# A searched order for a fused attention and gated-MLP kernel: no elementwise work on GpSimd, one float32 product for the first sums of squares, new tables

## The chip, the cores and the metric

One core of one Trainium2 chip. The metric is the device time of one execution in microseconds, the median over runs. The core's engines are PE (TensorE, matmuls), DVE (VectorE), ACT (ScalarE), POOL (GpSimd) and SP (SyncE, which here issues DMAs).

## The reference

Two parts, in float32. Attention over 8 batches, 8 heads, 576 positions and 64 dimensions, with a mask of its own for each half of the heads; then a gated MLP over the 4608 tokens x 512 features that come out:

```python
scores = q @ k.T / sqrt(64)               # masked with -1e9:
#   heads 0-3: 0 <= row - col < 32        heads 4-7: row >= col and row % 32 == col % 32
attn = softmax(scores) @ v                # -> x, 4608 tokens x 512
xn = x / sqrt(mean(x*x) + 1e-6) * rms_g
g, val = xn @ w_gate, xn @ w_val          # 512 x 1536 each
out = (g * sigmoid(g) * val) @ w_out      # 1536 x 512
```

## The kernel before, in words

**Numbers.** A large product is made in three matmuls: each operand is split into a high part (a cast to fp32r) and a low part (source minus high part), and high x high, low x high and high x low are summed. `split` (L584) does it: a copy that casts, by ScalarE or VectorE (`copyop`, L576, `copy_to`, L579), and a subtraction by VectorE or GpSimd (`elementwise`, L573; the instruction is recorded at L589). The helper `elementwise` also makes the additions and subtractions of L1201, L1022, L1029, L748, L762, L886 and L995.

**Attention.** 32 units, each one pair of heads of one batch. `unit_s` (from L664) makes a unit's scores in blocks of 64 columns (L699, L705: 72 or 36 short matmuls), the mask and maximum (L737, L740), the subtraction of it (L748), the exponential (L749), the row sum (L750), its reciprocal (L753, L754), the scaling (L762) and the transpose (L763). `unit_o` makes the values (L784, L797) and evacuates them (`evac`) into the chunk's rows. Units 0 to 3 form the lead-in; the others are put into the MLP's stages at places that the tables WIN, SAT, OAT, PSAT and POAT name.

**The MLP.** Nine chunks of 512 tokens. Chunks 0, 1 and 2 are computed plainly: for each of 12 blocks u of the hidden dimension the gate product (`slot_g`, L1077; in chunk 0 the first at L1085), the value product (L1077), and with a lag the output product (`slot_o`, L1132), 12 matmuls each. During chunk 0 the weights are read, unpacked on ScalarE and VectorE (`convert_weights`, L981 to L995) and split. Chunks 3 to 8 run as three pairs (`pair_of_chunks`) with a scheme of seven block products in place of eight; a block's products are called "5", "6", "2", "3", "7", "1", "4" (L1244, six matmuls each), and the outputs (L1373) follow, while the next pair's operands are made (`first_x`, `other_x`). Each chunk's RMS factor needs the sum of squares over features: `square` squares and adds up, `rms` sums over partitions with a product by ones. For chunk 0 it is four float32 products by ones, one per block of 128 features (L869), that accumulate in bank a1; `root0` follows.

**Order.** Nothing is issued as it is written. Each operation is registered by `op(engine, cost, ...)` with its reads and writes; `also=` names other engines that may do it. `Plan.forward` then simulates the engines with these costs (`act(n)`, `dve(n)`, `pool(n)`, SCO and PVO for scores and values, LATC for the latency between engines, TAIL) and at each step issues, on the engine that is free first, the ready operation with the lowest due time. The due times (DUE) and the slots in on-chip memory (PLACE) are two long tables found by a search. From chunk 1 on PE's operations keep the order in which they are written (`plan.serial`). Where the plan sees PE idle for long in the lead-in, filling matmuls on zeros are put in (`fill`, L603). The bytes of the tables are not shown.

Of the kernel before, what the change touches and what calls it, by code (L numbers as in the profile page):

```python
# [25 lines left out]
P = 128  # L26
# [27 lines left out]
MOVE = 60  # L54
# [5 lines left out]
SCO = (1340.0, 1050.0)  # L60
PVO = (1450.0, 1220.0)
# [6 lines left out]
TRA = 170.0  # L68
# [15 lines left out]
    "4028384c00041410061c352d585c591a1e40570b1b5b32045d4e211a50232e3d5319520c283840040814341c0c39155d3c3001393a04442400564d2f"  # L84
    "5a481c202c5d1814243c3854560f4004515a5d58551c3c140c2c4b5440004f585d494a1c14401c4c405618512c4c565455384a54484b512f59525c48"
    "49574b56544e4c1c502f53544e0e2e182d514f4c0c185d554c5b18400c534e5d2e510e2d2e402e3850530d4f50542e383853502e0c544a515d4e4e50"
    "542f4e180e1c2e545355512e0c0e1c50515b0d0c1e402e57564855545953495c4a1d401f1c2e2e50515839112c584a1c5a581f4d5c28525c1e2e524a"
    "18583618180e505a321c5c513410501d0f4b4a3832081f505a321036342458510e1e13045a44300c1e3758230b515a330b421c2943250e3c1e070d54"
    "3d3e16035a26341a2440001b3727350130020542314552321f120a0904153f10064c49232c4420224e53415149203211214a56284e581f2a4e163958"
    "36154f1323121454484a0a202b47492006085b3f22524a214c2d0c17592c1815582a2f0f2256575145171c5311554812143f5d4c2c5151221f58064d"  # L90
    "1d5910190b3909082253365b380a0f4d580a575309412d5d3f23462f2a2d125b444539323817143b182d513a194d1f2f3a28583b53490b230f090c57"
    "394d045336135810452d2b44194712481f4d1d18581138393a460f383348475836464804093b3809321c5a030641573f512a19314442450210430c28"
    "13001e0e1a3d2b07353c585a57510d30253e034127323f51110634181b1c3705443104471d241f0f132833460c0029104558095a1a11511232430e42"
    "2b010602075d2a531e343c03273f351621150d495119045b114740133741314f1f264855181b24363e4c0c1a590f10010646580212535d3515280017"
    "3d333f1d1c424e0e302a522529324d2b564307444554055c470327040d3c2f5851145b12363953110a233534595c021e162013075a144149222d5819"
    "15232f4a505c4c08122c4717105d4b442e3951080d16062d0f2304542c242e2d0a092159201e16120850375c513b0522365d4b4035455419353e0408"
    "272f2c1a2f494b4720505c110308405d204b3b535d161e530c08063b412459075b2f51153c46532e114605010803454750151a455d2e02343e13513c"
    "442e4516081e590f084c530c16105144411508075b12590d44271322531550040554061940485249245d290e18304f1e1c1101434d28033c2625553e"
    "5644515b15591d2904414c1b3f1a1f31490200074e48590f2a3d151c404d11332b2a1e4353520c285127323c425515181d121005543113060056264f"
    "1a3b292325024c1a09142a015241581b5d19403f0f040d202b1e494853210c113430223e425c560e513718354f033c10503233392d543d5929271d1c"  # L100
    "2c052813241f0706124e3643314d002655042f5a2e0844565d47092544505c0b524b0a423b3a1646394a0c17394a3c233e035b35505a025725385d58"
    "14562a4b000f50114d4c0151305726561a3a0416340b36523e515c4742371b45352a4434554d50464351023b1438102658164708110b5d554056251b"
    "0441471544190c09585c4f183f44570155000b0a0e18305d36513e0b35231a31555c4f46265641553c15512e1455175d03173f180016223b31345001"
    "1a092f4735144218263e46041a572a373036580f40430c1102102b271e543f4e23252053410e1f032c3d070d18473601112f51580c483c292e2d2105"
    "1c55493754503e201d4f2559061302331f4232002a311618011030030c34124d403f4e430e0d232235563a50412855534902360f37262b3d073c5c13"
    "211131011e42592d2c330551062f0401555847"))
DUE = np.frombuffer(bytes.fromhex(
    "024d0cf7017e01760cb00d6201b300070040002b018f0d4e0002016c000400000008021800050001000e0290000f0003007300430032001d001a0036"
    "016200ce02090052007500420093015c00940187010f01070022002a00390051007e001003da007a00230018000d02c400460071017b006a00d30014"
    "00170020004a001b0006009c0129012801fc01c40120000a0030004e003e004700290013000b000c010d00e6022401ab0100000900d900fd02750304"  # L110
    "02d600db00e701f400f9015800e4012400c1013b00c2010800bd00cb0069016900ed0207013f025c019500ad02b0009b011c01a900be00dc00a700b7"
    "006600aa01a0005900ae00b6005c011f0249025e00b1020e0193020a027a041401a10159021e00bc01540148010201a8009101e20406028a016b0142"
    "010400d000c700f600bb011e00a300920065006400280045011600a6011a019c002c009f005e010c018801840189021402280223013a0095005b007c"
    "01660127012e0080004b01ba02c001b901e50084028c01c0025a0164021c01d702f2012c033d022f02d301ed015e0230020201a70179033002690123"
    "011905d100f700e100fa00ea027b01da02760305012f0021001e00150016005d01fd02c8017d035002df0027001900240054015b01be025d02330212"
    "01460242020501b0014001ef01d200ec00eb002d0055003b024e021b016001c8033201b40149028d0165019f024701b602ad014f0229018101470286"
    "0206020b0231029e025102a801f2021101c5029c014d026d03aa01c9025501ee014a01cd02950172024a028902fa026401ad01c2034701f002cb0201"
    "0194048a02b5027e023c028801cf030a01f7034f024f02b80284035d02ea01c7026f01ae011b019b022d016801f8019801510296018a01cb01c60334"
    "014301750294031d0267015a01fa027c01dc02a502bf00f200dd00ff02b600df014b01d001a2030d02d201a301b20243032703e102570291021a0241"
    "01f50244025601e1024501e301df020f028e028301ea028f0279019701ca02250208028702c900d4029f01bd0232013701800280018e0250020d01a4"  # L120
    "01d500cc01ff0266026c027d0220027802b20215013803b902dc016f026501de023701530260029b02a100c001d1006c019d023d02e5031501c1025f"
    "027001c302e2020c0183031901e9016e0392029801f901d80254018b03a102210234024b013902ac039502a901d403d2014401e401f602a202aa013d"
    "029200fb037701bf027301fb036c02ae018d016d012a02a300ca004f025b017001ec04f3026a00780088004c010b041d023a0353010601e0019e01db"
    "02fc034e03860367022c02b301a503e4033f01ce03ba00f501d302ca029d03110452029a01e7023902cd037502a6021f01e803410177028202c302ff"
    "037802f10309016a02a4031802b702d101cc01f30302026e039002be02f802d503830272026303100385035803e7035902c10217014c029302e000f1"
    "035603310344028b022202ab038a0337035a0487039c02d80322047803e00363034903f40306066a05c304ee05b303c5034502ec03ca0407031f0468"
    "047b02610372041e032e0271021d0131041902bd02360252019902de01b701350117041b04430238057404ef05b80641031a02b103b800f3032d0404"
    "02f3025803b201d604bb0321012b00d2013600c6026b00f40113015600a10394041f037a038404c5036d03e902ef03c00083008d031303680325008b"
    "02fb02da036b035b008e00720374049c060a052a056503bd03b6036003fe044d042c0411039a02f4052804480063035203b3040902e601aa03c8036a"
    "03b4046302f6034a0307023b038d034206cd04d0058f069703d102e903cb037003290371030f034d03ce04e102f902f0040c025901860134031b0155"  # L130
    "022701030105010900cd03c7028103a7009d04e80465037c017a0362009e00600477055b065a048805f403a403ef02cc035402ed03f0048403550533"
    "03c104e60379030e0328022b03570346054c047d03ee037d03bf043c00d6004900740079039d0076008900a0004d00350061038002ee0323003a04d3"
    "032f02ba03de03ed00820050045505f605e60666003403b002c204aa038c03f702d7023e0277041603a0038f03fa033c049b037f041c03d802a00396"
    "050e0423039e03120361043905ff0597055605fe053b054d042e03d50433045c043604a80494051e049a03eb030c039803e503ab0403039704790434"
    "04100435032a033a03e203bc035e044b030b0338019a025302460491017403c3037b02e4024003e303200457036f062b02e10572053005b2051003bb"
    "0369042100c9046103ae0301042403000482032c04660196013e01d9024802ce0216042b00d100fe00b20097041803e8046900d50483045d03d00387"
    "006200a2045f06ce06c3064906be03d30343057002a7043e055306d804f5044704d6046000570210015f022a043101330182015d019000bf00a900c8"
# [102 lines left out]
PEN = {"DVE": 0.0, "ACT": 0.0, "Pool": 0.0}  # L240
# [189 lines left out]
def attn_moe(ctx: ExitStack, tc: tile.TileContext, qz: bass.AP, qT: bass.AP, kT: bass.AP, vz: bass.AP, vl: bass.AP,  # L430
# [129 lines left out]
    def dve(n, rate=0.96):  # L560
        return 150 + n / rate
# [1063 lines left out]
```

## Time and profile before

| | |
|---|---|
| median of three runs | 935.15 us (935.1 to 937.07) |
| the profiled execution | 937.66 us, span 935.9 us |
| PE busy | 915.2 us (98%), 8406 matmuls |
| PE weight loads | 738.3 us (79%) |
| DVE busy | 709.0 us (76%), 1083 instructions |
| ACT busy | 478.8 us (51%), 824 instructions |
| POOL busy | 145.4 us (16%), 115 instructions |
| DMA | 209.08 MB, mean 223 GB/s |
| mean granted TensorE clock | 0.996 |

The span runs from the first to the last instruction of the profiled execution; the time also has what lies around it. Busy time is the time in which an engine has at least one instruction in work. In the slices of the page PE is at nine tenths or more in all but the first and the last of forty. The chain of work that ended last lies on PE for 91% of the span and on DVE for 5%. The first matmul starts at 1.64 us, PE's first stretch without a gap at 39.21, and the last matmul ends near 931.2 us; two copies and two stores of 128 KB follow it.

### The profile page before, as it was taken

To read this page: it belongs to the slowest core of one execution; us is meant where nothing else is said; L and a number is where in the kernel's file an instruction comes from. 1 tells how busy PE (TensorE), PEld (TensorE's weight loads), DVE (VectorE), ACT (ScalarE), POOL (GpSimd) and SP (SyncE) were. 2 spreads that over 40 slices of the span, in tenths; PEclk is the share of its full clock that TensorE was granted. 3 is DMA by queue.
4 is the path that set the end of the run, shared out by engine and by line. 5 is a ranking of instruction groups with operands and counts; after the bars stand their busy time and mean duration, and the time that the engine had idled before them with its cause. 6 is when DMAs were issued, how large, how long until landed. Compare 5 with 4: busy or idle time off the path is not lost.

```text
span 935.9 us, 20718 instructions
## 1 busy us (share of the span) xinstructions
PE 915.2 (98%) x8406; PEld 738.3 (79%) x8406; DVE 709.0 (76%) x1083; ACT 478.8 (51%) x824; POOL 145.4 (16%) x115
## 2 busy tenths in 40 slices
PE   7899999999999999999999999999999999999997
PEld 4587788887878788888887887888888878888886
DVE  5999988878898878875678989554689984347781
ACT  6797764355445445454456672443466633233530
POOL 0112300100141410301025211000141120010200
PEclk9999999999999999999999999999999999999999
DMA  9966737879769549795646659964444698624642
GB/s 344 363 254 248 258 141 259 285 254 312 248 225 324 177 146 329 244 314 167 203 125 196 215 184 329 346 192 139 124 123 156 209 374 297 202 67 132 214 140 79
DMA packets 122655, 209.08 MB, mean 223 GB/s; under 512 B 10816, under 2 KB 66368, under 8 KB 119488
## 3 DMA queue, kind: packets, MB, share of 16 engines
q1 hardware_dynamic: 121840, 207.17, 66.0%
q8 instruction: 66, 1.08, 0.5%
q10 hardware_dynamic: 720, 0.59, 0.2%
q14 instruction: 29, 0.24, 0.1%
HBM read 163.68 MB, written 44.04 MB: 222 GB/s over the span
## 4 chain that ended last, share of the span: by engine, by line
PE 91%; DVE 5%; DMA 2%; issue 1%; ACT 0%; ACTq 0%; SPq 0%; DVEq 0%
PE a L1244 16%; PE g L1244 11%; PE v L1244 10%; PE a L1132 10%; PE g L1077 10%; PE v L1077 10%; PE a L1373 8%; PE v L1373 4%; PE g L1373 4%; PE pair L699 2%; PE pair L784 2%; DVE bl L589 1%; DMA xq<-in_qz_dram 1%; PE pair L797 1%; DMA few<-in_gain_dram 1%
## 5 line engine op out<-in xcount | busy, mean ns | idle before, releaser
L581 ACT CAST bl<-bl 128x512 fp32r<-128x512 f32 (+1 forms) x171 | 113.1, 685 | 107.4 <-DVE bl L1201 27.5
L1244 PE MATMUL a<-bl,bl 128*128 128x512 f32 x637 | 159.5, 394 | 0.0
L589 DVE TENSOR_TENSOR bl<-bl,bl 128x512 fp32r<-128x512 f32 x186 | 136.7, 758 | 16.1 <-ACT bl L581 4.8
L1244 PEld LDWEIGHTS a<-bl,bl 128*128 128x128 f32 x637 | 118.2, 188 | 25.5
L589 POOL TENSOR_TENSOR bl<-bl,bl 128x512 fp32r<-128x512 f32 x34 | 50.9, 1501 | 386.2 <-ACT bl L581 107.1
L1132 PE MATMUL a<-bl,bl 128*128 128x512 f32 x432 | 110.8, 394 | 0.0
L1244 PE MATMUL g<-bl,bl 128*128 128x512 f32 x426 | 109.0, 390 | 0.0
L1077 PE MATMUL g<-bl,bl 128*128 128x512 f32 x408 | 106.2, 400 | 1.0 <-DVE bl L1095 1.0
L1077 PE MATMUL v<-bl,bl 128*128 128x512 f32 x420 | 106.7, 392 | 0.2 <-DVE bl L1112 0.2
L1244 PE MATMUL v<-bl,bl 128*128 128x512 f32 x413 | 106.4, 390 | 0.0
L1255 DVE TENSOR_TENSOR a<-a,bl 128x512 f32<-128x512 f32 x72 | 50.2, 697 | 57.5 <-PE a L1244 44.0
L1132 PEld LDWEIGHTS a<-bl,bl 128*128 128x128 f32 x432 | 79.9, 188 | 17.2 <-DVE bl L589 0.3
L1201 DVE TENSOR_TENSOR bl<-bl,bl 128x512 f32<-128x512 f32 x103 | 72.8, 716 | 27.1 <-ACT bl L1260 25.8
L1244 PEld LDWEIGHTS g<-bl,bl 128*128 128x128 f32 x426 | 79.8, 188 | 16.7
L1077 PEld LDWEIGHTS v<-bl,bl 128*128 128x128 f32 x420 | 79.0, 188 | 17.6 <-DVE bl L1112 0.6
L1077 PEld LDWEIGHTS g<-bl,bl 128*128 128x128 f32 x408 | 76.1, 190 | 18.8 <-issue 1.6
L1244 PEld LDWEIGHTS v<-bl,bl 128*128 128x128 f32 x413 | 77.5, 188 | 16.3 <-ACT bl L1251 0.2
L1373 PE MATMUL a<-bl,bl 128*128 128x512 f32 x298 | 71.4, 390 | 0.0
L1373 PEld LDWEIGHTS a<-bl,bl 128*128 128x128 f32 x298 | 55.8, 188 | 11.7
L1373 PE MATMUL g<-bl,bl 128*128 128x512 f32 x208 | 50.1, 391 | 1.4 <-DVE bl L1393 1.4
L583 DVE CAST bl<-bl 128x512 fp32r<-128x512 f32 (+1 forms) x86 | 42.2, 494 | 12.0 <-PE a L1373 2.7
L1373 PE MATMUL v<-bl,bl 128*128 128x512 f32 x208 | 49.9, 390 | 0.7 <-DVE bl L1393 0.7
(175 smaller groups left out, 1318.7 us busy)
## 6 DMA issues: line engine op xcount, KB each, us to landing
bl<-gvd SPq DMA_DIRECT2D x252, 256.0 KB, 4.2
gvd<-bl SPq DMA_DIRECT2D x72, 256.0 KB, 4.3
bl<-to SPq DMA_DIRECT2D x72, 256.0 KB, 4.2
bl<-wos SPq DMA_DIRECT2D x54, 256.0 KB, 3.4
bl<-wos SPq DMA_DIRECT2D x12, 1024.0 KB, 6.5
bl<-in_wgv_dram SPq DMA_DIRECT2D x11, 1024.0 KB, 6.1
vt<-in_vl_dram SPq DMA_DIRECT2D x24, 352.0 KB, 3.7
xk<-in_kT_dram SPq DMA_DIRECT2D x28, 288.0 KB, 4.5
```

Of the source, the lines that this page charges most:

```text
L581: nc.scalar.copy(out=o, in_=i)
L583: nc.vector.tensor_copy(out=o, in_=i)
L589: elementwise(CH, lambda e: both(e).tensor_tensor(out=lo.new(F32R), in0=src(), in1=hi.f32(), op=ALU.subtract), reads + [hi.key], [lo.key])
L699: nc.tensor.matmul(out=pr[at // CH][32 * r:32 * r + 32, at % CH:at % CH + KW], lhsT=tq()[hd, q0:q0 + 32], rhs=tk_()[hd, q0:q0 + KW], start ...
L784: nc.tensor.matmul(out=ends[r % 2][0][n][64 * h:64 * h + 64, at + 32 * lo:at + 32 * hi], lhsT=va()[32 * r:32 * r + 32, D * (6 * n + j):D * ...
L797: nc.tensor.matmul(out=pr[s][64 * h:64 * h + 64, 32 * lo:32 * hi], lhsT=va()[r:r + 32, D * kb:D * kb + D], rhs=pT[r:r + 32, 64 * kb - 32 * ...
L1077: nc.tensor.matmul(out=out_, lhsT=w.t[:, sl], rhs=x.t, start=(kc == 0 and i == 0), stop=(kc == KC - 1 and i == 2))
L1132: nc.tensor.matmul(out=acc[t], lhsT=x.t[:, sl], rhs=w.t, start=(u == 0 and i == 0), stop=(u == NU - 1 and i == 2))
L1201: elementwise(CH, lambda e: both(e).tensor_tensor(out=o.new() if fresh else o.t, in0=a.t, in1=b.t, op=how), [a.key, b.key], [o.key])
L1244: nc.tensor.matmul(out=banks[bk], lhsT=w, rhs=xs[k][y].t, start=start and k == 0 and i == 0, stop=stop and k == 1 and i == 2, skip_group_c ...
L1255: op("DVE", dve(CH), 0, lambda: nc.vector.tensor_tensor(out=banks[bk], in0=banks[bk], in1=t.t, op=ALU.add), reads=[t.key], writes=[bk])
L1373: nc.tensor.matmul(out=banks[bks[j]], lhsT=v, rhs=xs[k][y].t, start=start and k == 0 and i == 0, stop=stop and k == KT - 1 and i == 2, ski ...
```

## The change

- `elementwise`, and the squares, no longer offer GpSimd as an engine: `also=[]`. GpSimd keeps its memsets and one copy of one column (L969).
- Chunk 0's squares go the way of the other chunks: one square stays as the accumulator, the other three are added to it (by `elementwise`), and a single float32 product by ones makes the sum (`square`, with p == 3).
- In chunks 1 and 2 a unit's loads stay where they were and its scores come after the block's gate product (`slot_g`) in place of ahead of it; in chunk 0 as before. In the pairs the scores come after product "2" in place of "6", one product later.
- The planner's costs: `act`, `dve`, SCO, PVO, TRA, LATC, `evac`, `copyop` and others have new numbers; scores and values get a new figure `soon` (SOON) by which their results are taken as ready earlier. MOVE and SQP go.
- PLACE and DUE have new contents. They change which slot a tile lies in, the order on each engine, which engine does an operation with a choice, and where `fill` is put.

```diff
-SCO = (1340.0, 1050.0)
-PVO = (1450.0, 1220.0)
+SCO = (1400.0, 1200.0)
+PVO = (1525.0, 1310.0)
+SOON = ((209.0, 171.0), (313.0, 234.0))
-TRA = 170.0
+TRA = 95.0
-LATC = 150.0
+LATC = 45.0
...
-            done = s + cost + self.TAIL[e]
+            done = s + cost + self.TAIL[e] - self.soon[i]
...
     def act(n, psum=False):
-        return (170 if psum else 195) + n / 1.2
+        return (55 if psum else 95) + n / 1.2 + 70 * (n > CH)
     def dve(n, rate=0.96):
-        return 150 + n / rate
+        return 70 + n / rate
...
     def elementwise(cost, fn, reads, writes):
-        op("DVE", dve(cost), 0, fn, reads=reads, writes=writes, port=True, also=[("Pool", pool(cost), True)])
+        op("DVE", dve(cost), 0, fn, reads=reads, writes=writes, port=True, also=[])
...
-        if c == 0:
-            sq = take()
...
-            hold.append((p, sq))
-            while p == 3 and hold:
-                n, s = hold.pop(0)
-                op("PE", SUM, 0, lambda n=n, s=s: nc.tensor.matmul(out=acc[1], lhsT=ones1.broadcast_to([P, P]), rhs=s.t, start=n == 0, stop=n == 3),
-                   reads=["ones", "pv3", s.key], writes=["a1"], pad=acc[1] if n == 0 else None)
-                give(s)
-            return
...
-        op("ACT", act(CH), 0, fn, reads=[rt.key], writes=[sq.key], also=way("i", ("DVE", dve(CH), True), ("Pool", pool(CH), True)))
+        op("ACT", act(CH), 0, fn, reads=[rt.key], writes=[sq.key], also=way("i", ("DVE", dve(CH), True)))
...
+        if c == 0 and p == 3:
+            s = ssq.pop(0)
+            op("PE", SUM, 0, lambda: nc.tensor.matmul(out=acc[1], lhsT=ones1.broadcast_to([P, P]), rhs=s.t, start=True, stop=True),
+               reads=["ones", "pv3", s.key], writes=["a1"], pad=acc[1])
+            give(s)
...
-                    if m == "6":
+                    if m == "2":
                         attention_s(u)
...
                     load(i)
                     load_v(i)
+                    if c == 0:
+                        unit_s(i)
+            slot_g(c, u)
+            for i, a in zip(WIN[c], SAT[c]):
+                if a == u and c:
                     unit_s(i)
-            slot_g(c, u)
```

## Rows read from the trace of the kernel before

**Rows 1.** The page, busy: us (share of span) xinstructions.

```profile
PE 915.2 (98%) x8406; PEld 738.3 (79%) x8406; DVE 709.0 (76%) x1083; ACT 478.8 (51%) x824; POOL 145.4 (16%) x115
```

**Rows 2.** Waits of PE: line, who ended it, total us, times, longest.

```profile
PE pair L699 <- issue: 2.2, 1, 2.2
...
PE g L1373 <- DVE bl L1393: 1.4, 1, 1.4
...
PE g L797 <- issue: 1.1, 1, 1.1
...
PE g L1077 <- DVE bl L1095: 1.0, 1, 1.0
...
PE v L1373 <- DVE bl L1393: 0.7, 1, 0.7
PE pair L797 <- issue: 0.7, 1, 0.7
PE v L784 <- DVE bl L1112: 0.7, 1, 0.7
PE pair L784 <- issue: 0.5, 1, 0.5
```

**Rows 3.** Timeline: start, us, engine line op out<-in xcount [idle before <-releaser].

```profile
555.03 0.68 DVE L589 TENSOR_TENSOR bl<-bl,bl 128x512 fp32r<-128x512 f32 x1
...
558.47 4.68 POOL L589 TENSOR_TENSOR bl<-bl,bl 128x512 fp32r<-128x512 f32 x3 [27.50 <-ACT bl L581]
558.51 1.80 DVE L589 TENSOR_TENSOR bl<-bl,bl 128x512 fp32r<-128x512 f32 x1 [0.87 <-ACT bl L581]
...
561.93 1.77 DVE L589 TENSOR_TENSOR bl<-bl,bl 128x512 fp32r<-128x512 f32 x1
```

**Rows 4.** The page, costliest groups: the subtraction (busy, mean ns).

```profile
L589 DVE TENSOR_TENSOR bl<-bl,bl 128x512 fp32r<-128x512 f32 x186 | 136.7, 758 | 16.1 <-ACT bl L581 4.8
...
L589 POOL TENSOR_TENSOR bl<-bl,bl 128x512 fp32r<-128x512 f32 x34 | 50.9, 1501 | 386.2 <-ACT bl L581 107.1
```

**Rows 5.** Timeline of PE around 321 us.

```profile
320.63 0.76 PE L699 MATMUL pair<-xk,xq 64*32 64x64 f32 x52
323.55 0.41 PE L699 MATMUL pair<-xk,xq 64*32 64x64 f32 x20 [2.17 <-issue]
```

**Rows 6.** DMA from 321.0 to 321.2 us: queue, packets, MB, share.

```profile
q8 instruction: 1, 0.02, 29.3%
```

**Rows 7.** Chain that ended last, 320 to 340 us: start, us, what.

```profile
323.97 4.40 PE g L1077 x12
...
335.29 2.72 PE g L1077 x12
```

**Rows 8.** Windows: length, busy PE, PEld, DVE, ACT, POOL (xcount), PEclk, DMA, GB/s.

```profile
30.00:40.00 10.00, 8.51 (x104) 5.46 (x105) 9.62 (x11) 10.00 (x16) 0.00 (x0) 1.00 0.83 319
40.00:130.00 90.00, 88.79 (x759) 71.14 (x758) 83.24 (x103) 69.62 (x80) 21.22 (x10) 1.00 0.66 242
```

**Rows 9.** Timeline of PE: the fourth float32 product, two passes.

```profile
40.75 1.02 PE L869 MATMUL a<-bl,ones 128*128 128x512 f32 x2
```

**Rows 10.** Timeline from 264 us: one unit, probabilities to values.

```profile
269.67 2.37 DVE L753 TENSOR_SCALAR st<-st 128x9 f32<-128x9 f32 x1
...
275.36 0.77 DVE L763 STREAM_TRANSPOSE pT<-pp 128x576 f32<-128x576 f32 x1
...
276.98 0.27 PE L784 MATMUL pair<-pT,vt 32*64 32x64 f32 x1
```

**Rows 11.** Timeline of VectorE ahead of the values at 522.8.

```profile
513.81 1.78 DVE L589 TENSOR_TENSOR bl<-bl,bl 128x512 fp32r<-128x512 f32 x1
515.52 1.84 DVE L748 TENSOR_TENSOR pp<-pp,st 128x576 f32<-128x576 f32 x1
...
521.91 0.78 DVE L763 STREAM_TRANSPOSE pT<-pp 128x576 f32<-128x576 f32 x1
```

More of the change, by code (lines that the diff above doesn't have):

```diff
@@ L53 @@
 MID = 2
-MOVE = 60
 BYROW = ()
@@ L262 @@
     LAT = LATC
-    TAIL = {"PE": 165.0, "DVE": 90.0, "ACT": 110.0, "Pool": 60.0, "SP": 0.0}
+    TAIL = {"PE": 165.0, "DVE": 90.0, "ACT": 110.0, "Pool": 100.0, "SP": 0.0}
     def __init__(self):
@@ L278, in __init__, with op @@
         self.pads = []
+        self.soon = []
         self.owner, self.picked, self.uses = {}, [], []
-    def op(self, eng, cost, at, fn, reads=(), writes=(), bytes_=0, rel=0.0, lock=(), tab=None, port=False, chain=False, also=None, early=0.0, follow=None, pad=None):
+    def op(self, eng, cost, at, fn, reads=(), writes=(), bytes_=0, rel=0.0, lock=(), tab=None, port=False, chain=False, also=None, early=0.0, follow=None, pad=None, soon=0.0):
         i = len(self.ops)
         self.pads.append(pad)
+        self.soon.append(soon)
         self.early.append(early)
@@ L573, in elementwise @@
     def elementwise(cost, fn, reads, writes):
[L574 removed]
+        op("DVE", dve(cost), 0, fn, reads=reads, writes=writes, port=True, also=[])
     def copyop(fn, reads, writes):
[L577 removed]
+        op("ACT", act(CH), 0, fn, reads=reads, writes=writes, also=[("DVE", 340, True)])
     def copy_to(e, o, i):
@@ L717, in peak @@
                 nc.vector.tensor_scalar(out=mx, in0=mx, scalar1=0.125, scalar2=None, op0=ALU.mult)
-            op("DVE", dve(SW) + (170 if keys_ == [SK] else 330), 0, peak, reads=keys_, writes=[sk])
+            op("DVE", dve(SW) + (220 if keys_ == [SK] else 330), 0, peak, reads=keys_, writes=[sk])
             if i in HALFQ:
@@ L754, in recip @@
             nc.vector.reciprocal(out=su, in_=su)
-        op("DVE", 430, 0, recip, writes=[sk], port=True)
+        op("DVE", 400, 0, recip, writes=[sk], port=True)
         if i in ROWS:
@@ L801, in unit_o @@
             keys_ = ends[0][1] + ends[1][1]
-        op("PE", PVO[eight] + (SLOWV if i < 4 else 0), 0, values8 if eight else values, reads=tkeys + kv, writes=keys_ + ["pv3"] * (i == 3), pad=pr[1])
+        op("PE", PVO[eight] + (SLOWV if i < 4 else 0), 0, values8 if eight else values, reads=tkeys + kv, writes=keys_ + ["pv3"] * (i == 3), pad=pr[1], soon=SOON[eight][1])
         give(*held, *y)
@@ L847, in unit_o @@
                 n = z1 - z0
-                op("ACT", act(n, True) + MOVE * (len(moves) - 1), 0, evac, reads=ek, writes=list(dict.fromkeys(s.key for s, _, _ in moves)),
-                   also=way("e", ("DVE", dve(n) + 80 * (len(moves) - 1), False)))
+                op("ACT", len(moves) * 55 + n * (1 / 1.2 if p < 2 else 1.4), 0, evac, reads=ek, writes=list(dict.fromkeys(s.key for s, _, _ in moves)),
+                   also=way("e", ("DVE", len(moves) * 70 + n * (1 / 0.96 if p < 2 else 1.4), False)))
         square(b, p)
@@ L954, in copyop2 @@
     def copyop2(fn, reads, writes):
-        op("ACT", act(2 * CH), 0, fn, reads=reads, writes=writes, also=[("DVE", 150 + 2 * 274, True)])
+        op("ACT", act(2 * CH), 0, fn, reads=reads, writes=writes, also=[("DVE", 605, True)])
     raws = []
@@ L1459, in half @@
                     copy_to(e, (dst.new() if lead else dst.t)[:, sl], banks[P2[j]][:, sl])
-                op(e, 310, 0, half, reads=[P2[j]] + [dst.key] * (not lead), writes=[("oh", c, j, n)] + [dst.key] * lead)
+                op(e, act(256, True) if e == "ACT" else dve(256), 0, half, reads=[P2[j]] + [dst.key] * (not lead), writes=[("oh", c, j, n)] + [dst.key] * lead)
                 op("ACT" if n == 0 and not more else "SP", 600 if n == 0 else 430, 0, lambda sl=sl, dst=dst, q=q, j=j: (nc.sync if more else q).dma_start(
```

291 lines of the change are left out of this document (142 added, 149 removed).

## Prediction

> **What bounds the kernel now.** I read the page's busy shares first. PE is busy for 915.2 of 935.9 us, DVE for 709.0, POOL for 145.4 [rows 1]. The matmuls follow one another without a gap nearly everywhere, so apart from PE work that is taken out, all that can be won is PE's waits, the lead-in and the tail. The waits of PE come next, because they name who ended each one [rows 2]. Four of them, 1.4, 1.0, 0.7 and 0.7 us, end on a VectorE operation; two, 2.2 and 0.5 us, and three more in the lead-in (0.7 to 1.1 us) end on "issue", which means on nothing that the profile shows.
>
> Why is VectorE late in those four? The timeline ahead of the 1.4 us wait shows it [rows 3]. A subtraction of 512 columns takes 0.68 us at 555.03. At 558.47 GpSimd starts three of the same kind that last 4.68 us together, and beside them three VectorE operations in a row, each of 512 columns, take 1.80 to 1.77 us (the first and the last are shown). The two engines don't add up: what GpSimd works, VectorE loses in part. Over the run GpSimd takes 1.50 us for such a subtraction and VectorE's own 186 average 0.758 us [rows 4], 0.078 above the undisturbed one, which is 14.5 us on that line alone.
>
> The longest wait stands inside one unit's scores: 52 small matmuls go out, nothing for 2.17 us, then the other 20 of the same tile [rows 5]. They read the operands of the first 52, so it is not data. In the 0.2 us from 321.0, just ahead, the instruction queue carries one packet [rows 6]; I read the wait as PE running out of instructions after values and scores, two bursts of short matmuls with only six long ones between them. It costs twice: the next twelve matmuls take 4.40 us, twelve of the same kind later 2.72 [rows 7], a clock at half its level (1.2 instead of 2.4 GHz) for a while after the idle time.
>
> **The change part by part.** The sum is made against the profiled execution, 937.66 us with a span of 935.9 (1.8 lie around it); the median of the three runs is 935.15, 2.5 below, and I take the difference over to it.
>
> 1. *GpSimd's elementwise work goes to VectorE.* 103 or so of GpSimd's 115 instructions are of this kind [rows 1]. At 0.68 us each VectorE gains at most 70 us, and at least 14.5 come back: 709 becomes 764 or less, 82% of the span. The four waits lose what made VectorE late. Bounds: 0, if VectorE's longer queue makes it as late again, and -3.8 us, their sum. I take -3.8: in the 1.4 us case, VectorE would have the three GpSimd subtractions (2.0 us at its own length) to do in place of stretches of 1.1 us on three operations (3.3). Next late there would be ScalarE's cast, on which each subtraction waits.
>
> 2. *The first 130 us, where VectorE has least room.* From 40 to 130 us it is busy 83.2 of 90 us and GpSimd runs ten of its operations [rows 8]. At VectorE's length these are 6.8 us, as much as is free; a stretch of 1.1 us returned for half of them is 5.5. So VectorE's net is +1.3 to +6.8, and PE, without a gap there but for 1.2 us, pays between 0 and +6.8. I take +1.0, near the lower end: the casts can still move from VectorE to ScalarE, which is busy 69.6 of those 90 us.
>
> 3. *One product for the sums of squares in place of four.* A float32 product takes 1.02 us from its start to its end [rows 9], and three go: -3.1 at most. Only the later ones fall where PE has no idle time (from 30 to 40 us PE is busy 8.5 of 10 us). In exchange three additions of 512 columns, 0.68 us each, come onto VectorE, busy 9.6 of 10 us there, with ScalarE at 10.0 [rows 8]: 0 to +2.0, and the single product waits for the last addition. Bounds -3.1 and +2.0; I take 0 for both together (-1.0 and +1.0).
>
> 4. *Scores behind the gate product (chunks 1 and 2), and one product later in the pairs.* Twelve long matmuls, 2.72 us, now stand between one unit's values and the next unit's scores, ahead of the six that stood there. That spreads the two bursts. The wait of 2.17 us and the 1.68 us of slow clock behind it go: bounds 0 and -3.9. I take -3.9, since the move separates exactly the two bursts around it.
>
> 5. *The price of 4.* Scores 2.72 us later (12 units), or six matmuls later in the pairs (1.36 us), leave less time until the values product, whose place on PE is fixed. One unit's transpose ends at 276.13 and its values begin at 276.98, 0.85 us of room [rows 10]: 1.9 us would be missing. But its chain holds an operation on nine columns that took 2.37 us beside GpSimd, when 576 columns take 0.77; at least 1.6 come back. The last unit of the first pair has no room (transposed at 522.69; PE waited 0.5 us) and would miss 1.4 us more, yet two operations ahead of it took 1.78 and 1.84 us beside GpSimd [rows 11], 2.2 too much. Bounds -0.5 and +3.3; I take +0.5. Ahead of the moved scores PE holds the gate product, behind them the value product and the output products, in a fixed order; VectorE's mask of the scores waits for them, and nothing else.
>
> 6. *Shorter lengths for VectorE and ScalarE in the planner, the new tables of order and slots, finer evacuation costs.* They change no work. The order decides PE's waits and the lead-in; bounds -4.0 (the three "issue" waits of the lead-in, 2.5 by their ends of 0.7 and 1.1, and the 1.5 us that PE idles from 30 to 40) and +3, what a second refill wait of 2.2 us with part of its slow clock would cost. I take 0.
>
> Sum: -3.8 + 1.0 + 0 - 3.9 + 0.5 + 0 = -6.2. The profiled execution would be 931.5, the median 935.15 - 6.2 = 929.
>
> The Trainium skill speaks against step 4. "Runtime: NRT & Kernel Launch", section "Instruction fetch mechanics", says that the sequencer fetches the next block of instructions while it executes the current one, and that crossing a block is mostly hidden. By that the move wins nothing; the packet at 321.0 with the wait behind it says that here it was not hidden, once. The trace as a whole agrees with "mostly": long matmuls show no such wait.
>
> **The rivals.**
>
> *A: the refill wait stays or comes back at another unit.* For it: three more "issue" waits stand in the lead-in, and in the pairs scores and values still come in bursts. Against it: only one of 24 units in the body had it at this length. All terms but step 4's gain hold: -6.2 + 3.9 = -2.3, 933. This is also what the page's rule gives.
>
> *B: slower. VectorE becomes the bound in the first 130 us.* Place: the conversion of the weights, where VectorE and ScalarE feed PE. The point: the 6.8 us that VectorE has free from 40 to 130 us are used up; beyond that each us on VectorE is one on PE, with 1.7 us more of slow clock after a wait of about 2 us. Price: 6.8 (no stretch returned) + 2.0 (additions) and two slow stretches, 3.4, is +12.2. Against it stand 3.8 - 1.0 = 2.8 from the waits elsewhere, 3.9 from step 4, 1.0 from step 3, less 0.5 of step 5: +12.2 - 7.2 = +5, 940. For it speaks VectorE's 9.6 of 10 us; against it the stretches returned and the room on ScalarE.
>
> *C: the order is better in the lead-in too.* -6.2 - 4.0 = -10.2, 925. For it: real lengths are what an order has to fit. Against it: VectorE at 96% and ScalarE at 100% from 30 to 40 us.
>
> *D: the change does not do what it says:* waits of the old order go and others come in the new one, as many: 935. For it: 98% on PE is the result of such a search already.
>
> **Chances.** Forecast 0.50 (929, own range 925 to 932.5), A 0.14, B 0.12, C 0.13, D 0.11. A measurement of this kernel can tell 0.2%, 1.9 us, from no change: below 933.3 is faster, above 937.0 slower. Forecast and C are faster, A in two of three cases and D in one of ten: 0.50 + 0.13 + 0.10 + 0.01 = 0.74. D otherwise and the rest of A lie within: 0.04 + 0.08 = 0.12; B and the upper edge of D are slower: 0.14. The range, 922 to 937, takes in A, C and D and leaves out most of B and C's far side.
>
> **What would show it.** Right: no elementwise row on POOL; VectorE's L589 mean near 0.69 and its busy time between 730 and 764; no PE wait above 0.5 us on VectorE after 90 us; no "issue" wait of 2 us in the body and the clock row full from 300 to 350 us. One pair of L869 records in place of four. Step 2 is wrong if PE's busy share from 40 to 130 us falls under 0.97, step 5 if values products (L784) wait for a transpose. The prediction fails if PE stands idle for over 6 us between 40 us and the tail, or if its first gapless stretch begins more than 3 us later than now.

## The result, and the profile after

| | before | after |
|---|---|---|
| median, same chip | 935.95 us (935.1 to 937.07, 4 runs) | 925.99 us (924.88 to 926.88, 4 runs) |
| ratio | | 0.9892, 95% interval 0.9875 to 0.9909 |
| the profiled execution, span | 937.66, 935.9 us | 925.99, 924.1 us |

The forecast was 929 with a range of 922 to 937, and the change is faster: the direction holds, the gain is 10 us in place of 6.2. The time lies nearer to rival C (925) than to the forecast.

The page of after, busy times, and its row of the subtraction, which answer to [rows 1, 4]:

```profile
PE 910.3 (99%) x8392; PEld 735.0 (80%) x8392; DVE 731.6 (79%) x1173; ACT 480.3 (52%) x842; POOL 1.2 (0%) x12
...
L590 DVE TENSOR_TENSOR bl<-bl,bl 128x512 fp32r<-128x512 f32 x220 | 145.4, 686 | 9.7 <-PE v L1235 3.1
```

VectorE makes 34 more subtractions than before in only 8.7 us more, because each takes 686 ns in place of 758. Over all its work it is busy 22.6 us longer, for 90 more instructions.

Waits of PE in after, which answer to [rows 2]:

```profile
PE v L604 <- POOL still L600: 1.6, 1, 1.6
...
PE g L798 <- issue: 1.1, 1, 1.1
...
PE a L798 <- DVE bl L764: 0.9, 1, 0.9
...
PE v L1068 <- DVE bl L1103: 0.6, 1, 0.6
PE a L1068 <- DVE bl L986: 0.5, 1, 0.5
...
PE pair L785 <- issue: 0.2, 1, 0.2
```

The four waits on VectorE and the one of 2.2 us are gone. What is left above 0.2 us lies before 76 us.

Windows of after (length, then busy time and count of PE, PEld, DVE, ACT, POOL, then PEclk, DMA share, GB/s), beside [rows 8]:

```profile
30.00:40.00 10.00, 8.34 (x65) 5.80 (x64) 9.97 (x13) 9.92 (x11) 0.00 (x0) 1.00 1.03 408
40.00:130.00 90.00, 89.25 (x782) 70.75 (x781) 88.07 (x117) 71.91 (x82) 0.00 (x0) 1.00 0.70 255
130.00:376.00 246.00, 246.00 (x2876) 199.23 (x2875) 220.83 (x358) 119.61 (x213) 0.00 (x0) 1.00 0.74 247
376.00:900.00 524.00, 523.67 (x4092) 427.36 (x4091) 387.26 (x634) 256.07 (x452) 0.00 (x0) 1.00 0.64 208
```

From 40 to 130 us VectorE is now busy 88.07 of 90 us and PE still 89.25, more than the 88.79 of before. From 130 us PE has no idle time worth a name.

Busy shares don't say where time is won. For that I compare PE's position: the k-th long matmul of a line starts in the one trace earlier (minus) or later (plus) than the k-th of that line in the other. In chunk 0 the order of the matmuls differs, so the first row is read just behind it. The differences from before to after, and to the first experiment below, split by stretches of before:

| stretch of before, us | after | GpSimd's work on VectorE alone |
|---|---|---|
| 0 to 140, lead-in and chunk 0 | -3.77 | -1.61 |
| 140 to 302 (wait at 278) | -0.92 | -0.92 |
| 302 to 341 (wait at 321) | -3.95 | -1.84 |
| 341 to 514 | +0.30 | +2.77 |
| 514 to 585 (wait at 568) | -2.39 | -2.27 |
| 585 to the last matmul | -0.07 | -0.41 |
| behind the start of the last matmul | -0.93 | -0.88 |
| sum (difference of the spans) | -11.74 | -5.16 |

The last row but one is nearly the same in both: from the start of the last matmul to the end of the stores it takes 5.10 us in before (also in experiments 3 and 7), 4.17 in after and 4.22 in experiment 1. No step forecast it, and why is open. The medians of before and after are 1.7 us closer than the profiled times.

### The profile page after: what moved, and what is told of

Its sections match the earlier page's. It is cut to its first block, busy times and chain, and to the rows that moved or that the text cites. A ratio compares the mean times of both kernels' runs of the same rounds, so it can differ in the third digit from the quotient of the medians.

```text
span 924.1 us, 20561 instructions
## 1 busy us (share of the span) xinstructions
PE 910.3 (99%) x8392; PEld 735.0 (80%) x8392; DVE 731.6 (79%) x1173; ACT 480.3 (52%) x842; POOL 1.2 (0%) x12
## 4 chain that ended last, share of the span: by engine, by line
PE 89%; DVE 4%; DMA 4%; ACT 2%; issue 1%; SPq 0%; ACTq 0%; DVEq 0%
PE a L1235 16%; PE g L1235 10%; PE v L1235 10%; PE a L1123 9%; PE v L1068 9%; PE g L1068 9%; PE a L1364 8%; PE g L1364 5%; PE v L1364 5%; PE pair L700 2%; PE pair L785 2%; DMA bl<-in_wo_dram 1%; DVE bl L982 1%; DVE bl L980 1%; DMA bl<-in_wgv_dram 1%; PE pair L798 1%
## 5 line engine op out<-in xcount | busy, mean ns | idle before, releaser
L590 DVE TENSOR_TENSOR bl<-bl,bl 128x512 fp32r<-128x512 f32 x220 | 145.4, 686 | 9.7 <-PE v L1235 3.1
L582 ACT CAST bl<-bl 128x512 fp32r<-128x512 f32 (+1 forms) x169 | 107.5, 665 | 87.5 <-DVE bl L1192 16.1
L1192 DVE TENSOR_TENSOR bl<-bl,bl 128x512 f32<-128x512 f32 x124 | 84.0, 688 | 34.9 <-ACT bl L1251 33.1
L1068 PE MATMUL v<-bl,bl 128*128 128x512 f32 x420 | 109.4, 397 | 0.7 <-DVE bl L1103 0.6
L1235 PE MATMUL v<-bl,bl 128*128 128x512 f32 x417 | 107.4, 391 | 0.0
L1364 PE MATMUL v<-bl,bl 128*128 128x512 f32 x213 | 50.6, 389 | 0.0
L1242 ACT COPY bl<-g 128x512 f32<-128x512 f32 x36 | 21.1, 587 | 51.1 <-PE g L1235 49.6
```

The costliest lines, as they stand in the source:

```text
L582: nc.scalar.copy(out=o, in_=i)
L590: elementwise(CH, lambda e: both(e).tensor_tensor(out=lo.new(F32R), in0=src(), in1=hi.f32(), op=ALU.subtract), reads + [hi.key], [lo.key])
L1068: nc.tensor.matmul(out=out_, lhsT=w.t[:, sl], rhs=x.t, start=(kc == 0 and i == 0), stop=(kc == KC - 1 and i == 2))
L1192: elementwise(CH, lambda e: both(e).tensor_tensor(out=o.new() if fresh else o.t, in0=a.t, in1=b.t, op=how), [a.key, b.key], [o.key])
L1235: nc.tensor.matmul(out=banks[bk], lhsT=w, rhs=xs[k][y].t, start=start and k == 0 and i == 0, stop=stop and k == 1 and i == 2, skip_group_c ...
L1242: op("ACT", act(CH, True), 0, lambda: nc.scalar.copy(out=t.new(), in_=banks[bk]), reads=[bk], writes=[t.key])
```

## The experiments

Each of the three sets ran beside the kernel before on one chip: 936.05, 936.53 and 935.89 us. Line numbers of an experiment are shifted by some 10 to 40 against the kernel it comes from. Most of the diffs are excerpts: lines that carry the due times along when operations move or are added are left out.

**1. GpSimd's operations on VectorE, nothing else.** The order of before stays word for word.

```diff
     def both(e):
-        return nc.vector if e == "DVE" else nc.gpsimd
+        return nc.vector
```

> The kernel before with its plan, costs and tables unchanged; only what the plan gives to GpSimd is issued on VectorE, at the same place of the order. Theory (GpSimd stretches VectorE, and that ended four PE waits): VectorE's 512-column subtraction averages 0.69 us instead of 0.758, its busy time rises from 709 to about 747 us, the PE waits at 93, 278, 568 and 755 us go (3.8 us in all), the time falls by 1 to 4 us, to 932 to 935. Rival (VectorE has no room): its busy time rises to over 764 us, new PE waits on VectorE of over 4 us come, above all from 40 to 130 us, and the time is 938 or more.

Measured: 932.51 us, ratio 0.9966 (0.9954 to 0.9977). Its waits of PE, and its subtraction on VectorE:

```profile
PE pair L716 <- issue: 1.9, 1, 1.9
```

```profile
L606 DVE TENSOR_TENSOR bl<-bl,bl 128x512 fp32r<-128x512 f32 x220 | 145.3, 685 | 13.6 <-ACT bl L598 3.7 <-PE a L1390 2.6 <-PE v L1390 1.6
```

The subtraction is at 685 ns, and the waits at 93, 278, 568 and 755 us are gone, so GpSimd's work was what made VectorE late there. Whether by its stretch or by its own late results, experiment 2 asks. VectorE's busy time is 726.7 us and not the 747 expected: more came back than the 14.5 us of the one line. Without GpSimd, though, the old order loses 2.77 us between 341 and 514 us, and the issue wait stays.

**2. GpSimd beside VectorE for nothing.** In the kernel after, every second `split` gets a subtraction on GpSimd beside it, into a buffer that nobody reads. The order of PE, VectorE and ScalarE is word for word that of after.

```diff
+        count[0] += 1
+        if count[0] % 2 == 0:
+            nc.gpsimd.tensor_tensor(out=junk, in0=hi.f32(), in1=hi.f32(), op=ALU.subtract)
```

> The kernel after, and beside every second subtraction of split (99 in all) GpSimd subtracts the same 512 columns into a buffer that nobody reads; the order of PE, VectorE and ScalarE is word for word that of after. Theory (GpSimd stretches VectorE's operations beside it): GpSimd busy about 150 us, VectorE's busy time +25 to +45 us over 731.6, the mean of its subtraction from 686 to 740 to 800 ns, PE waits on VectorE come back, 928 to 931. Rival (what made VectorE late was the late result of GpSimd, not the stretch): VectorE's mean stays below 700 ns and the time at 926 plus or minus 1.

Measured: 966.25 us, ratio to before 1.0315 (1.03 to 1.0331), 40 us over after. The page, and groups of VectorE and GpSimd (busy, mean ns, idle before):

```profile
PE 922.7 (96%) x8392; PEld 735.9 (76%) x8392; DVE 795.7 (83%) x1173; ACT 479.9 (50%) x842; POOL 162.8 (17%) x122
```

```profile
L614 DVE TENSOR_TENSOR bl<-bl,bl 128x512 fp32r<-128x512 f32 x220 | 183.8, 861 | 8.8 <-PE v L1259 3.2 <-PE a L1147 1.5 <-ACT bl L599 1.4
L1270 DVE TENSOR_TENSOR a<-a,bl 128x512 f32<-128x512 f32 x72 | 50.0, 696 | 60.8 <-PE a L1259 52.2 <-ACT bl L1275 8.0
...
L608 POOL TENSOR_TENSOR junk<-bl 128x512 f32<-128x512 f32 x110 | 161.6, 1469 | 768.7 <-DVE bl L601 418.3 <-ACT bl L599 234.1 <-issue 96.0
```

VectorE's busy time grows by 64.1 us beside 161.6 us of GpSimd that gives nothing to anyone; the subtraction goes from 686 to 861 ns. The rival (late results of GpSimd) falls as the only cause, since no result is used here, and no wait of PE, VectorE or ScalarE ends on one of the added operations. My sizes were too small: 25 to 45 us of VectorE and 2 to 5 us of time were expected, 64 and 40 came, nearly all of the time behind 370 us (+3.1 there). There PE's longest waits are for VectorE's subtractions (L1388 on L614: 4.9 us in five waits).

VectorE's own additions with a source in PSUM (L1270) stay at 696 ns, as in after (698). The Trainium skill ("SBUF — State Buffer", section "Who interferes with whom") says that a VectorE instruction with two SBUF inputs contends with a GpSimd instruction that reads SBUF; both rows agree with it.

**3. Other boundaries of instruction blocks.** In the kernel before, 40 matmuls of 64 columns on zeros take the place of 5 filling matmuls in the lead-in. That adds 70 PE instructions ahead of the body.

```diff
-        for _ in range(n):
+        for _ in range(n - 5 * (not tiny)):
             nc.tensor.matmul(out=pad[:, CH - FILLN:CH], lhsT=still[:, 0:P], rhs=still[:, 0:FILLN], ...)
+        while len(tiny) < 40:
+            tiny.append(nc.tensor.matmul(out=pad[0:64, 0:64], lhsT=still[0:64, 0:64], rhs=still[0:64, 0:64], ...))
```

> The kernel before with 40 matmuls of 64 columns on zeros put into the lead-in, in the place of five of its filling matmuls, where PE waits for the first operands: 70 PE instructions more ahead of everything else, and nothing else changed. Theory (the 2.17 us wait inside the scores at 321 us is the refill of PE's instructions, which came due just there because values, six matmuls and scores lay in one block): with the blocks shifted by 70 instructions the wait is gone, the twelve matmuls after it take 2.72 us instead of 4.40, and the time falls by 3.9 us, to 932. Rival (the wait belongs to that unit: its bank, its operands, the transfers around it): 2.2 us stay at the same matmul, 935 to 936.

Measured: 936.59 us, ratio 1.0004 (0.9994 to 1.0014). Waits of PE:

```profile
PE a L817 <- issue: 2.7, 1, 2.7
PE pair L719 <- issue: 2.4, 2, 1.5
```

The first row lies in the lead-in, at 22 us. The wait at 321 us is gone, and two others stand inside scores, near 224 and 294 us; with them the time stays, and the 932 of the expectation did not come. No data had changed, only the count of instructions ahead. So the wait is a refill: PE has used up its block of instructions before the next block's packet is in, and the place of the wait goes with the count.

Counted in PE's records (matmuls, weight loads and waits on semaphores), PE runs dry within two records of 448 + 256n. Counted over the body, the shortest stretch in which 256 successive PE instructions start is 2.96 us in before, at five units of chunks 1 and 2, and 4.22 us in its pairs. In after it is 5.15 us. In before the packet of the block that was late came 3.0 us behind the last boundary, and PE went on 2.4 us later: 5.4 us for a block that was used up in 3.1. At the two waits here it is 4.1 and 4.8 us, for blocks used up in 3.2 and 3.3.

**4. The scores moved, nothing else.** Costs, due times and slots of before; each moved operation keeps its due time.

```diff
             for i, a in zip(WIN[c], SAT[c]):
                 if a == u:
                     load(i)
                     load_v(i)
-                    unit_s(i)
+                    if c == 0:
+                        unit_s(i)
             slot_g(c, u)
+            for i, a in zip(WIN[c], SAT[c]):
+                if a == u and c:
+                    unit_s(i)
...
-                    if m == "6":
+                    if m == "2":
                         attention_s(u)
```

> The kernel before with only the scores moved (behind the gate product in chunks 1 and 2, behind product 2 in the pairs); costs, due times and slots as before. Theory (instructions run out where two bursts of short matmuls meet): the wait of 2.2 us at 321 us and its slow clock go, PE's position between 302 and 328 us improves by 3.5 to 4.0, no issue wait of 2 us in the body; against it stands up to 1 us of waits for units that are ready later. 932 to 933, ratio about 0.9965. Rival A (the wait comes back at another unit): another issue wait of 1.5 to 2.4 us in the body and 935 to 936. Rival on step 5 (units too late): waits of PE on VectorE ahead of values products of over 3 us together, 935 or more.

Measured: 956.44 us, ratio 1.0211 (1.019 to 1.0232). PE's position gains 4.0 us between 302 and 341 us, as forecast, and no issue wait is left in the body. Then the pairs lose 25 us. The two longest waits of PE there, and VectorE ahead of the first:

```profile
PE pair L801 <- DVE pT L780: 6.1, 1, 6.1
PE a L1261 <- DMA bl<-gvd: 4.2, 1, 4.2
```

```profile
702.48 0.21 DVE L771 RECIPROCAL st<-st 128x9 f32<-128x9 f32 x1
...
708.65 4.79 DVE L606 TENSOR_TENSOR bl<-bl,bl 128x512 fp32r<-128x512 f32 x6
...
717.44 2.75 DVE L1218 TENSOR_TENSOR bl<-bl,bl 128x512 f32<-128x512 f32 x4
720.11 0.77 DVE L780 STREAM_TRANSPOSE pT<-pp 128x576 f32<-128x576 f32 x1
```

The unit's reciprocal is done at 702.7 (its scaling, on GpSimd, at 704.0) and its transpose starts at 720.11, behind a row of subtractions and additions that the old plan put ahead of it. At this wait the price of the later scores is set by VectorE's order, not by the unit's own operations. It is 6.1 of the 25 us; what delays the other waits was not followed.

**5. Two of the edits, in chunks 1 and 2 alone.** Experiment 1, and the scores moved in chunks 1 and 2 but not in the pairs.

```diff
-        return nc.vector if e == "DVE" else nc.gpsimd
+        return nc.vector
...
-                    unit_s(i)
+                    if c == 0:
+                        unit_s(i)
             slot_g(c, u)
+            for i, a in zip(WIN[c], SAT[c]):
+                if a == u and c:
+                    unit_s(i)
```

> The kernel before with two edits: GpSimd's elementwise operations issued on VectorE, and the scores moved behind the gate product in chunks 1 and 2 alone (not in the pairs, not the sums); old costs, due times and slots. Theory (stretch and refill are separate and add up; the pairs' move is not needed for either): 936.3 - 3.4 - 3.8 = 929, ratio 0.992, no issue wait of over 1 us in the body, PE's position -1.6 at the end of chunk 0, about -5.5 at 328 us and -7 to -8 at the end. Rival (the moved scores need the new tables in chunks 1 and 2 as they did in the pairs): 932 or more, with PE waits on VectorE between 130 and 376 us.

Measured: 931.66 us, ratio 0.995 (0.9932 to 0.9968); 929 was expected. The refill's 3.96 us are won, and 1.4 are lost between 177 and 277 us, most of it at 204 us, where PE waits 0.93 us for VectorE's copies of a unit's values out of the bank that the gate product needs: the rival's kind of wait, a short one. The rest of the gap is overlap: experiment 1 already had 1.84 of those 3.96, because its wait of 1.9 us was not followed by a slow clock. Windows of the kernel before and of experiment 1 behind the wait:

```profile
323.50:328.50 5.00, 4.95 (x33) 3.95 (x33) 3.37 (x6) 0.09 (x1) 0.00 (x0) 0.66 0.70 238
```

```profile
322.00:324.00 2.00, 2.00 (x11) 1.64 (x9) 2.00 (x5) 0.00 (x0) 0.00 (x0) 1.00 0.82 273
324.00:326.00 2.00, 2.00 (x10) 1.69 (x9) 1.39 (x4) 1.78 (x2) 0.00 (x0) 1.00 0.88 244
```

**6. One product for the sums, planned anew.** The kernel before with three additions and one product, the additions with the due time of their square.

```diff
+            op("DVE", dve(CH), 0, lambda: nc.vector.tensor_tensor(out=acc_.t, in0=acc_.t, in1=sq.t, op=ALU.add), ...)
...
-                op("PE", SUM, 0, lambda n=n, s=s: nc.tensor.matmul(out=acc[1], ..., rhs=s.t, start=n == 0, stop=n == 3), ...)
+                op("PE", SUM, 0, lambda: nc.tensor.matmul(out=acc[1], ..., rhs=s.t, start=True, stop=True), ...)
```

> The kernel before with one part of the change: three additions on VectorE and one float32 product in place of four products, the other due times and slots as they were. Theory (three products of 0.87 to 1.0 us go from an engine that has no gap from 39 us on): output matmuls of chunk 0 come 1 to 3 us earlier and the time is 933 to 935. Rival (VectorE and ScalarE set the lead-in, and the three additions, 2.0 us, come onto them): PE's first gapless stretch begins 1 to 2 us later and the time is 936 to 938.

Measured: 953.68 us, ratio 1.0195 (1.0177 to 1.0213). The wait at the product:

```profile
PE a L887 <- DVE bl L883: 8.7, 1, 8.7
```

The additions had come too late in VectorE's order, so this run tells of the order and not of the product.

**7. The same with the order held.** An addition stands at the place of the second, third and fourth product, and the one product behind the last.

```diff
...
+                    if n:
+                        nc.vector.tensor_tensor(out=first.t, in0=first.t, in1=s.t, op=ALU.add)
+                    if n == 3:
+                        nc.tensor.matmul(out=acc[1], lhsT=ones1.broadcast_to([P, P]), rhs=first.t, start=True, stop=True)
```

> The kernel before with one product for chunk 0's sums: at the places of the second to fourth product an addition of 512 columns is issued on VectorE instead, and the one product stands at the place of the fourth; the order of everything else is word for word as before. Theory (forecast's step 3): the products that go stood in time in which PE waited anyway, the additions are paid on VectorE: PE's position at the end of chunk 0 within 1 us of before, 935 to 937. Rival 1 (three products are PE time): position -2 to -3 at the end of chunk 0, 933 to 934. Rival 2 (the product waits for the last addition on a full VectorE): a wait of PE over 1 us at the product, +1 to +3, 937 to 939.

Measured: 938.63 us, ratio 1.0023 (1.0011 to 1.0035); the position at the end of chunk 0 is +1.16. PE and VectorE at the product:

```profile
42.29 1.12 PE L893 MATMUL a<-bl,ones 128*128 128x512 f32 x2 [1.93 <-DVE bl L891]
```

```profile
41.55 0.68 DVE L891 TENSOR_TENSOR bl<-bl,bl 128x512 f32<-128x512 f32 x1
```

Three products fewer win nothing in the old order; the last addition costs a wait of 1.93 us. That is rival 2.

**8. Three products more, in after.** The single product is made four times over.

```diff
-            op("PE", SUM, 0, lambda: nc.tensor.matmul(out=acc[1], ..., start=True, stop=True), ...)
+            op("PE", SUM, 0, lambda: [nc.tensor.matmul(out=acc[1], ..., start=True, stop=True) for _ in range(4)], ...)
```

> The kernel after, with the single float32 product of chunk 0's sums made four times over (three times more, same place, same order of everything else). Theory (in the new order it stands where PE has work ready behind it): PE's position +3 (three times 1.02) from 33 us on, 929. Rival (forecast's step 3, it lies in time in which PE waits anyway): less than 1 us, 926 to 927.

Measured: 926.69 us, ratio to before 0.9898 (0.988 to 0.9916). PE from 30 to 40 us:

```profile
30.00:40.00 10.00, 10.00 (x67) 5.98 (x66) 9.97 (x13) 9.92 (x11) 0.00 (x0) 1.00 1.03 408
```

PE's idle time there, 1.66 us in after, is filled. The position is +1.4 at 37.6 us and +0.44 from 84 us on. So in the new order the three products by themselves are worth under half a microsecond; what their additions cost there stands in both kernels and is not measured.

**9. All three edits, old costs and tables.** First with GpSimd not offered in the plan (the first two lines), the scores of experiment 4 and the sums of experiment 6; then experiments 1, 4 and 7 in one.

```diff
-        op("DVE", dve(cost), 0, fn, reads=reads, writes=writes, port=True, also=[("Pool", pool(cost), True)])
+        op("DVE", dve(cost), 0, fn, reads=reads, writes=writes, port=True, also=[])
...
-                    if m == "6":
+                    if m == "2":
                         attention_s(u)
```

> The kernel before with all three edits of the work (no elementwise work on GpSimd in the plan, one product, scores moved) but its old costs and tables. Theory (the edits carry the gain): 926 to 930. Rival (the new costs and searched tables carry it): 932 or more, with PE waits of over 4 us in new places.

> The kernel before with all three edits of the work (no elementwise work on GpSimd, scores moved, one product as in the run above) but the old costs, due times and slots. Theory (the edits bring the gain, the new tables little): 936 - 3.4 (measured for the first) - 3.5 (scores) and 0 to -1 for the product: 928.5 to 929.5, and 2.5 to 3.5 us remain to the new tables. Rival (the new tables carry it): the edits disturb the old order and the sum is not reached: 931 to 936, with PE waits on VectorE of 1 us and more.

Measured: 1028.71 us (ratio 1.0989, 1.0961 to 1.1017) and 961.31 us (1.0256, 1.0233 to 1.0279). In the second the position is -3.8 at 328 us, with the refill won, and +25 at the end. Waits of PE in the first:

```profile
PE g L1262 <- DVE bl L606: 13.1, 2, 9.1
PE pair L801 <- issue: 11.8, 1, 11.8
PE a L887 <- DVE bl L883: 9.2, 1, 9.2
```

The second row is no refill, though the view puts it down to "issue": the packet of its block had come at 563.75 us, and PE goes on at 589.66, 0.10 us behind a transpose on VectorE (588.78, 0.78 long). All three edits together are no gain in the old order: without new due times they cost 93 and 25 us.

**10. After with other boundaries.** 50 short matmuls in place of 5 filling ones, in the kernel after.

```diff
-        for _ in range(n):
+        for _ in range(n - 5 * (not tiny)):
...
+        while len(tiny) < 50:
...
```

> The kernel after, with 50 matmuls of 64 columns on zeros in place of 5 filling matmuls in the lead-in: about 90 PE instructions more ahead of the body, so that every later boundary of a block of 256 instructions falls elsewhere. In after no 256 successive PE instructions of the body take less than 5.15 us (before: 2.96). Theory (moving the scores cured the refill wait, whatever the boundaries): no issue wait of 1 us or more after 40 us, PE's position within 0.5 us, 926 plus or minus 1. Rival (after is free of the wait by luck of its boundaries): an issue wait of 1 to 2.4 us in the body and 927 to 930.

Measured: 927.67 us, ratio to before 0.9908 (0.9889 to 0.9927). The one issue wait inside scores, and the instruction queue from 220.8 to 221.4 us (packets, MB, share):

```profile
222.20 0.82 PE L720 MATMUL pair<-xk,xq 64*32 64x64 f32 x60
223.55 0.33 PE L720 MATMUL pair<-xk,xq 64*32 64x64 f32 x12 [0.52 <-issue]
```

```profile
q8 instruction: 1, 0.02, 9.2%
```

A wait is still possible, but short: this packet came 3.9 us behind its boundary, the block lasted 5.6 us, and PE stood for 0.52 us; the position worsens by 0.7. So the move is a cure for most of it and not for all: in wait and position nearer to the first of my two theories, by the median (927.67) at the near end of the rival's 927 to 930.

**11. After with the pairs' scores one product earlier again,** their due times with them.

```diff
-                    steps[u][0](m)
                     if m == "2":
+                        n0 = len(plan.ops)
                         attention_s(u)
+                        n1 = len(plan.ops)
+                        steps[u][0](m)
+                        plan.swaps.append((n0, n1, len(plan.ops)))
+                    else:
+                        steps[u][0](m)
```

> The kernel after, with the pairs' scores again one product earlier (behind product 6), their due times with them. In the pairs of before no 256 PE instructions took less than 4.22 us and no refill wait was seen. Theory (in the pairs the move won nothing and cost about 0.5): 925.5, the 0.5 us at 415 to 436 us back. Rival 1 (the bursts of the pairs are short enough for a refill wait under other boundaries): an issue wait of up to 1.2 us with slow clock, 927 to 929. Rival 2 (the new order stands on the new place): waits on VectorE in the pairs, 928 or more.

Measured: 946.91 us, ratio to before 1.0128 (1.0096 to 1.0159). Waits of PE:

```profile
PE a L802 <- ACT bl L1268: 6.6, 1, 6.6
PE v L1252 <- DVE bl L1289: 5.9, 1, 5.9
PE a L802 <- DVE bl L1285: 2.2, 2, 1.9
```

No refill wait inside scores, and 20 us lost with nothing changed but the order, nearly all between 430 and 506 us. The tables of after fit their own place of the scores just as those of before fit theirs. Whether the pairs' move by itself won or cost anything can't be told from this; a search with the old place was not made.

## Why the prediction was right in direction and short by 4 us

1. *GpSimd's elementwise work to VectorE, -3.8: right.* The waits at 278, 568 and 755 us give -0.9, -1.7 and -1.0, the one at 93 -1.2 (experiment 1), together 4.8. The cause is shown from both sides: taken away in experiment 1, put back without any use in experiment 2. That experiment 1 as a whole comes out at -3.5 is luck, though: it also has 1.8 us of the refill wait, which was shorter and had no slow clock behind it, and loses 2.8 between 341 and 514 us. VectorE's 731.6 us lie at the low end of the 730 to 764.

2. *The first 130 us, +1.0: wrong side.* Moving the operations there won time even in the old order: experiment 1 is at -1.61 at 140 us, some -0.4 beyond the wait at 93. VectorE at 88.07 of 90 us held PE up no more than at 83.24. I had taken a full VectorE for a late one; its busy share doesn't tell whether the operation that PE waits for next is early in its queue.

3. *One product, 0: right.* +1.2 in the old order (experiment 7); in the new the three products are worth 0.4 (experiment 8), without the additions. Both lie inside the bounds.

4. *Scores moved, -3.9: right, to 0.1 us.* -3.95 in after, -4.0 alone (experiment 4), the mechanism by experiment 3. The Trainium skill's "mostly hidden" ("Runtime: NRT & Kernel Launch", section "Instruction fetch mechanics") holds for long matmuls in these traces: from 130 to 376 us in after, PE is busy all of 246.00 us. It fails where a block of 256 was used up in 3.1 to 3.3 us (before, experiment 3), and by 0.52 us once in one of 5.6 (experiment 10). The pairs' share of the move had no wait to win.

5. *The price of 4, +0.5: the size held (+0.30 from 341 to 514 us), the working did not.* I worked it out from the unit's own chain and its stretched operations. Experiments 4 and 11 show that the order decides: the move costs 25 us with due times that were not searched for it, and taking half of it back costs 20. That the size agrees is luck.

6. *New lengths and tables, 0: this is the step that failed.* "They change no work" is true, and still after lies some 5.4 us below experiment 5 (ratios 0.9892 and 0.995), which has the first edit and the refill's part of the fourth in the old order: more than either edit brought there. What else differs is the product, some 0.4, and the pairs' move. In the lead-in and chunk 0 after is 2.16 us ahead of experiment 1. The first 40 us show how: up to there PE has started 31 long matmuls of the MLP in after, 13 in experiment 1 and 12 in before, and in return fewer filling matmuls (18, 23 and 26), matmuls of scores (180, 216 and 207) and of the sums (2, 6 and 6). PE's order differs there. In after:

```profile
32.42 1.02 PE L876 MATMUL a<-bl,ones 128*128 128x512 f32 x2
32.88 1.72 PE L1076 MATMUL g<-bl,bl 128*128 128x512 f32 x5
...
38.62 5.51 PE L1068 MATMUL a<-bl,bl 128*128 128x512 f32 x23 [0.48 <-DVE bl L986]
```

The sum's product is done at 33.4 us, where before made its last at 40.75 [rows 9], and behind 38.62 long matmuls follow in a block of 23. Between 341 and 514 us the new order loses 0.30 where the old one, without GpSimd, lost 2.77. And it makes the pairs' moved scores affordable (experiments 4 and 9; in chunks 1 and 2 the move cost 1.4 in the old order, experiment 5). So the new tables' share is what is left when the rest is taken off; no experiment has them without the edits. Which of the costs, due times or slots does it can't be told apart: the tables belong to the costs they were searched with.

Of the rivals, B and D fall. A's mechanism is real (experiment 3) but in after leaves 0.5 us at most in the runs made. C is what happened beside the forecast: of its 4.0 us about half came in the lead-in. By the table the forecast is missed above all in the lead-in and chunk 0: -3.77, where it had 0 (+1.0 of step 2, -1.0 of the wait at 93). Of the rest, the stretch with the wait at 568 gave 1.0 more than its 1.4, the one behind it 0.6 less than its 0.7, and the 0.9 behind the last matmul stood in no step.

No run was faster than after; experiment 5, without new tables, gets 4.2 of its 10 us.

## What to carry to other kernels

Work given to a second engine is no gain if it stretches the first one's operations: compare the mean length of the same instruction with and without the neighbour before counting busy time. Where bursts of short instructions meet, count how long a block of 256 lasts against the time until the next block's packet has served, here 4.1 to 6.3 us at the waits of before and of experiments 1, 3 and 10. In a kernel whose order was searched, an edit and its order belong together: without a new order two edits won 0.3 and 0.5% (experiments 1 and 5), the others made the kernel 0.2 to 10% slower (experiments 4, 6, 7 and 9), and all with it made it 1.1% faster.

## What was not expected of the hardware

A refill wait of 2.17 us was followed by 5 us at a mean granted clock of 0.66, a mix of the two levels 1.2 and 2.4 GHz; waits of 1.9 us (experiment 1) and 1.5 us (experiment 3) at the same kind of place were followed by none. GpSimd's subtractions cost VectorE 0.58 us each (64.1 us over 110) even where they serve nobody, and an operation of VectorE with a source in PSUM none. One with a single input in SBUF is not spared: the 68 casts of 512 columns went from 425 ns in after to 511 in experiment 2. At the refill waits of before and of experiments 1, 3 and 10 the block's packet had come 1.7 to 3.9 us behind the start of the block that ran dry, and PE went on 2.3 to 2.5 us after the packet; elsewhere in before, behind 40 us, packets came from 4.4 us ahead of that start to 4.7 us behind it (by the count of records), and no wait followed.
